# Decoding float64 weights: the exponent shift as a scaled copy on ScalarE, the sign on GpSimd, the residual on VectorE

## The chip, the cores and the metric

One core of a Trainium2 chip. The metric is the device time of one execution in microseconds; the kernel before took 1084.58 us in the median of 3 runs (1082.89 to 1086.86).

## The reference

The input is 2304 tokens (4 sequences of 576), 8 heads of 64, model width 512. Three layers follow one another:

```python
scores = scale * q @ k.T                 # causal window of 128, a linear bias per head
attn = softmax(scores) @ v
h = x @ w_in;  r = relu(h);  y = (r * r) @ w_out          # w_in 512x2048, w_out 2048x512
logits = y @ w_gate + softplus(y @ w_noise) * noise
out = sum over the top 2 of 8 experts of weight * (relu(y @ w1[e]) @ w2[e])   # 512x1024, 1024x512
```

The weights w_in and w_out of the middle layer reach the kernel as float64 (seen there as pairs of int32 words); all else is float32.

## The kernel before

TensorE multiplies in a float32 form that keeps fewer bits, so every operand is split in two: a high part that ScalarE writes by a Copy into that form, and a low part that is the number less its high part. A product is then three matmuls (high by high, high by low, low by high). `mm1` (L123, matmuls at L128) is the first product of a layer, `mm2` (L131, L133) the second.

The middle layer's weights come in 16 chunks. `load_w_moe(f)` (L99) brings chunk f in two halves, u = 0 and 1, of 128 x 512 numbers, 32 halves in all. One half is a 512 KB transfer on SyncE's queue (L104) into `st`, whose words alternate: the low and the high 32 bits of each float64, so that `lo` and `hi` are read with a step of two words. From them the float32 `a` is made: L108 shifts the high word by 3 and masks it (mantissa and low exponent bits), L109 puts the sign and the top exponent bit in, L111 the three topmost bits of the low word. ScalarE squares the high word, read as a float32 (L114), and L115 multiplies `a` by whether that square reaches a bound, so that numbers under float32's range come out as 0. ScalarE copies `a` into the high part of `w` (L116) and GpSimd subtracts to give the low part (L117). `st` and `a` have three buffers each.

The work is one stream per engine. The program's order is that of the loops below, but the framework moves instructions of one engine past one another where the data allow it, before the program runs; on the chip each engine takes its queue in order. First the attention for the first two token tiles runs, with the weights of chunks 0 and 1 (L630 to L636). Then the loop at L641 takes step s from 0 to 19: `m_mm1` (L335) multiplies chunk s for token group 0 (256 tokens) and chunk s - 4 for group 1, chunk s + 2 is loaded and decoded (L646), the attention of the next token tiles is spread over the steps, and `m_mm2` (L350) does the second product of the step before. Inside `m_mm1` ScalarE makes the ReLU, its square and the high part of that (L342 to L344), and VectorE the low part (L345). Weights stay in on-chip memory, so the groups from 2 on (L669) decode nothing. Attention's instructions that the text names: the subtraction for the keys (L218), the scaling and the subtraction for the queries on GpSimd (L223, L226), the masked maximum (L264, L267), the division by the sum (L277 on GpSimd, L282 on ScalarE), the transposes (L290). L137 to L168 make constants, some with GpSimd's iota.

Of the kernel before, what the change touches and what calls it, by code (L numbers as in the profile page):

```python
# [8 lines left out]
F32 = mybir.dt.float32  # L9
# [4 lines left out]
AF = mybir.ActivationFunctionType  # L14
OP = mybir.AluOpType
# [7 lines left out]
def kernel(  # L23
# [11 lines left out]
    nc = tc.nc  # L35
# [24 lines left out]
    BIG = -2.56e11  # L60


    TINY = (1.0625 * 2.0 ** -15) ** 2

    const = ctx.enter_context(tc.tile_pool(name="const", bufs=1))
    dram = ctx.enter_context(tc.tile_pool(name="dram", bufs=1, space=bass.MemoryType.DRAM))
# [19 lines left out]
    def slot():  # L86
        pool = ring_a if nslot[0] // HR % 2 == 0 else ring_b
        nslot[0] += 1
        return pool.tile([P, 2, 2 * DM], F32R, name="w")

    def load_w(src):
        w = slot()
        st = m2.tile([P, 2 * DM], F32, name="wst", bufs=2)
        nc.sync.dma_start(out=st, in_=src)
        nc.scalar.activation(w[:, 0], st, AF.Copy)  # L95
        nc.vector.tensor_tensor(out=w[:, 1], in0=st, in1=w[:, 0].bitcast(F32), op=OP.subtract)  # L96
        return w

    def load_w_moe(f):  # L99
        w = slot()  # L100
        for u in range(2):
            c = slice(u * DM, (u + 1) * DM)
            st = s64.tile([P, DM, 2], I32, name="w64", bufs=3)
            nc.sync.dma_start(out=st.rearrange("p f t -> p (f t)"), in_=wm32[f, u])  # L104
            lo, hi = st[:, :, 0], st[:, :, 1]
            a = s64.tile([P, DM], I32, name="wa", bufs=3)
            af = a.bitcast(F32)
            nc.vector.tensor_scalar(a, hi, 3, 0x3FFFFFF8, op0=OP.logical_shift_left, op1=OP.bitwise_and)  # L108
            nc.vector.scalar_tensor_tensor(out=a, in0=hi, scalar=-0x40000000, in1=a,  # L109
                                           op0=OP.bitwise_and, op1=OP.bitwise_or)  # L110
            nc.vector.scalar_tensor_tensor(out=a, in0=lo, scalar=29, in1=a,  # L111
                                           op0=OP.logical_shift_right, op1=OP.bitwise_or)
            m = hi.bitcast(F32)
            nc.scalar.activation(m, m, AF.Square)  # L114
            nc.vector.scalar_tensor_tensor(out=af, in0=m, scalar=TINY, in1=af, op0=OP.is_ge, op1=OP.mult)  # L115
            nc.scalar.activation(w[:, 0, c], af, AF.Copy)  # L116
            nc.gpsimd.tensor_tensor(out=w[:, 1, c], in0=af, in1=w[:, 0, c].bitcast(F32), op=OP.subtract)  # L117
        slots["m", f] = w

    def load_w_exp(e, f):  # L120
# [510 lines left out]
    for _, i, j, fn in sorted(steps, key=lambda x: x[:3]):  # L631
        fn()
        if j == 0 and i + 2 < FT:
            a_load(i + 2)
        if j == 3:
            load_w_moe(i)  # L636
# [4 lines left out]
    for s in range(NFC + LATE):  # L641
        now = [(g, s - LATE * g) for g in range(2) if 0 <= s - LATE * g < NFC]
        for g, f in now:
            m_mm1(g, f)
        if s + 2 < NFC:
            load_w_moe(s + 2)  # L646
        if s < NA:
            for fn in afill[s * per:(s + 1) * per]:
                fn()
        if s == NA - 1:  # L650
            A["cm"].__exit__(None, None, None)
            ring_b = ctx.enter_context(tc.tile_pool(name="ring_b", bufs=HR, side="right", reuse_waits="tile"))
            a_pool("at", 2, qk=1, v=2, qt=1, sb=2, pt=1)
            a_load(FT - 1)
            a_qk(FT - 1, "k")
            a_load(FT)
            afill2 = a_pair(FT, False)
        elif s >= OFF and s - OFF < len(afill2) and afill2[s - OFF]:
            afill2[s - OFF]()
        for g, f in prev:  # L660
            m_mm2(g, f)
        prev = now
        if s == NFC - 1:
            s64_cm.__exit__(None, None, None)
            gp_cm = tc.tile_pool(name="gp", bufs=1)
            gp = gp_cm.__enter__()
# [100 lines left out]
    with tc.For_i(0, nov, 1) as t:  # L767
        with tc.For_i(0, E, 1) as e:
# [6 lines left out]
            for dst, src in ((xg, yd[:, :]), (old, out)):  # L775
                nc.gpsimd.indirect_dma_start(
                    out=dst, out_offset=None, in_=src,
# [12 lines left out]
            for f in range(NEC):  # L790
                w = load_w(w_flat[ds((e * NEC + f) * P, P), :])
# [6 lines left out]
                                               op0=OP.max, op1=OP.subtract)  # L798
# [3 lines left out]
                out=out, out_offset=bass.IndirectOffsetOnAxis(ap=ic[:, 0:1], axis=0),  # L802
# [59 lines left out]
```

## Time and profile before

| | before |
|---|---|
| median of 3 runs | 1084.58 us (1082.89 to 1086.86) |
| profiled execution | 1080.51 us |
| its span, first to last instruction | 1078.5 us |
| TensorE busy (matmul) | 1019.0 us |
| VectorE busy | 593.5 us |
| ScalarE busy | 508.8 us |
| GpSimd busy | 236.2 us |
| mean granted TensorE clock | 0.989 |

In the profile PE is TensorE, DVE is VectorE, ACT is ScalarE, POOL is GpSimd and SP is SyncE; PEld is the loading of a matmul's weights. A busy time is the sum of an engine's instructions over the span; the engines run beside one another. A letter q behind an engine's name (SPq) is its sequencer or queue. Each row names a line of the kernel, an engine, an operation, what is written and read (out<-in) and the shapes, partitions x elements per partition.

### The profile page before, as it was taken

The numbers are of one execution on the slowest core, as the hardware profiler recorded it, in microseconds if no ns is written. First come the engines' busy times: TensorE is split into PE (matmuls) and PEld (weight loads), VectorE is DVE, ScalarE is ACT, GpSimd is POOL, SyncE is SP. The second block draws the span as 40 slices with busy tenths as digits, with TensorE's granted clock in tenths as the row PEclk, the third lists the DMA queues.
The fourth block names the chain that finished last, engine by engine and source line by source line (L and its number), as shares of the span: only waits on it lengthen the run. The fifth ranks groups of instructions, "written<-read, shape, count | busy, mean of one in ns | idle before, by whom it ended". The sixth has DMA issues, their size and how long they took to land.

```text
span 1078.5 us, 17965 instructions
## 1 busy us (share of the span) xinstructions
PE 1019.0 (94%) x6636; PEld 879.8 (82%) x6636; DVE 593.5 (55%) x1732; ACT 508.8 (47%) x1272; POOL 236.2 (22%) x219
## 2 busy tenths in 40 slices
PE   4788989999999999999999998999999999999997
PEld 3657768778888888888887787898888898888885
DVE  8999994576555646555547555444343444342312
ACT  6776665655646556665647525333322232321110
POOL 2334341220201111110100103314141322222111
PEclk9998999999999999999999999999999999999999
DMA  6333441621011111110015605535353444432111
GB/s 231 101 118 119 136 128 61 228 60 31 30 31 50 30 40 40 40 30 31 12 59 152 211 17 178 183 104 168 98 169 117 146 126 132 145 105 71 40 51 46
DMA packets 36521, 104.18 MB, mean 97 GB/s; under 512 B 7527, under 2 KB 7783, under 8 KB 36432
## 3 DMA queue, kind: packets, MB, share of 16 engines
q1 hardware_dynamic: 27232, 75.72, 22.3%
q0 software_dynamic: 9200, 27.29, 8.0%
q8 instruction: 53, 0.87, 0.3%
q14 instruction: 36, 0.29, 0.1%
HBM read 86.02 MB, written 20.00 MB: 98 GB/s over the span
## 4 chain that ended last, share of the span: by engine, by line
PE 65%; DVE 13%; DMA 8%; issue 6%; ACT 6%; POOL 1%; SPq 0%; POOLq 0%; DVEq 0%; ACTq 0%
PE h L128 28%; PE y L133 25%; DMA old<-out_dram,idx 4%; PE t L133 3%; PE t L305 2%; PE y L250 2%; DMA wst<-in_w_exp_dram 1%; DVE gl L345 1%; ACT sb L271 1%; DVE sb L264 1%; DVE wa L115 1%; PE t L569 1%; DMA qks<-in_qk_dram 1%; PE t L290 1%; DVE wa L109 1%
## 5 line engine op out<-in xcount | busy, mean ns | idle before, releaser
L128 PE MATMUL h<-xh,w 128*128 128x256 f32 x1152 | 238.3, 290 | 11.4 <-ACT r L342 6.3
L128 PE MATMUL h<-xeh,w 128*128 128x304 f32 (+2 forms) x1024 | 229.5, 305 | 0.9 <-ACT xeh L572 0.9
L128 PEld LDWEIGHTS h<-xh,w 128*128 128x128 f32 x1152 | 190.4, 193 | 22.8 <-ACT r L342 8.0
L133 PE MATMUL y<-w,gh 128*128 128x512 f32 x576 | 189.9, 410 | 0.9 <-ACT gh L344 0.8
L128 PEld LDWEIGHTS h<-xeh,w 128*128 128x128 f32 x1024 | 171.4, 188 | 3.5 <-ACT xeh L572 1.1
L128 PE MATMUL h<-xl,w 128*128 128x256 f32 x576 | 164.9, 286 | 1.1 <-DVE xl L312 1.1
L96 DVE TENSOR_TENSOR w<-wst,w 128x1024 fp32r<-128x1024 f32 x64 | 78.4, 1225 | 148.9 <-ACT w L95 148.8
L128 PE MATMUL h<-xel,w 128*128 128x304 f32 (+2 forms) x512 | 154.8, 302 | 0.4 <-DVE wt L574 0.4
L133 PE MATMUL y<-w,hh 128*128 128x512 f32 x464 | 145.0, 393 | 0.0
L95 ACT ACTIVATE w<-wst 128x1024 fp32r<-128x1024 f32 x64 | 67.7, 1058 | 135.8 <-PE t L133 128.0
L588 ACT ACTIVATE hh<-h 128x304 fp32r<-128x304 f32 (+1 forms) x120 | 50.4, 420 | 147.5 <-PE h L128 146.6
L133 PE MATMUL y<-w,gl 128*128 128x512 f32 x288 | 115.2, 402 | 3.2 <-DVE gl L345 3.2
L133 PEld LDWEIGHTS y<-w,gh 128*128 128x128 f32 x576 | 100.1, 191 | 21.1 <-ACT gh L344 1.3
L128 PEld LDWEIGHTS h<-xl,w 128*128 128x128 f32 x576 | 111.1, 193 | 4.9 <-DVE xl L312 1.3
L342 ACT ACTIVATE r<-h 128x256 f32<-128x256 f32 x144 | 54.3, 377 | 126.0 <-PE h L128 79.5
L345 DVE TENSOR_TENSOR gl<-r,gh 128x256 fp32r<-128x256 f32 x144 | 69.1, 480 | 79.1 <-ACT gh L344 78.3
L589 DVE SCALAR_TENSOR_TENSOR hl<-h,hh 128x304 fp32r<-128x304 f32 (+1 forms) x120 | 55.9, 466 | 102.2 <-ACT hh L588 102.1
L541 POOL DMA_INDIRECT xg<-yd,idx x40 | 40.8, 1021 | 273.2 <-PE h L128 111.8
L128 PEld LDWEIGHTS h<-xel,w 128*128 128x128 f32 x512 | 96.4, 188 | 1.8 <-DVE wt L574 0.6
L133 PEld LDWEIGHTS y<-w,hh 128*128 128x128 f32 x464 | 83.9, 188 | 14.8
L133 PE MATMUL y<-w,hl 128*128 128x512 f32 x232 | 91.3, 393 | 0.0
L277 POOL TENSOR_TENSOR sb<-sb,rs 128x512 f32<-128x512 f32 x28 | 29.8, 1063 | 276.0 <-ACT sb L253 106.4
(191 smaller groups left out, 1643.9 us busy)
## 6 DMA issues: line engine op xcount, KB each, us to landing
wst<-in_w_exp_dram SPq DMA_DIRECT2D x64, 512.0 KB, 3.7
w<-in_w_moe_dram SPq DMA_DIRECT2D x32, 512.0 KB, 3.7
qks<-in_qk_dram SPq DMA_DIRECT2D x20, 512.0 KB, 3.7
vs<-in_v_dram SPq DMA_DIRECT2D x20, 256.0 KB, 2.7
yd<-ysb SPq DMA_DIRECT2D x18, 256.0 KB, 2.1
out_dram<-ysb SPq DMA_DIRECT2D x1, 4608.0 KB, 14.0
xg<-yd,idx POOLq DMA_INDIRECT x40, 3.7
out_dram<-old,idx POOLq DMA_INDIRECT x29, 2.8
```

The lines of the kernel that those rows point to most:

```text
L95: nc.scalar.activation(w[:, 0], st, AF.Copy)
L96: nc.vector.tensor_tensor(out=w[:, 1], in0=st, in1=w[:, 0].bitcast(F32), op=OP.subtract)
L128: nc.tensor.matmul(ps, w[:, wi, c], x[:, kk, :], start=(n == 0), stop=(n == 3 * KD - 1))
L133: nc.tensor.matmul(ps, g, w[:, wi, DM:], start=(start and n == 0), stop=(stop and n == 2))
L250: nc.tensor.matmul(sp[c][:, pp], a[r, p, :], b[r, p, s0:s0 + 2, :], start=(n == 0), stop=(n == 2))
L277: nc.gpsimd.tensor_tensor(out=sb, in0=sb, in1=r.to_broadcast([P, 2, 2, P]), op=OP.mult)
L305: nc.tensor.matmul(o[64 * c:64 * c + 64, pp, :], vv[n][:, 4 * hf + j, :], pts[n][:, j, :], start=(n == 0), stop=(n == 1))
L342: nc.scalar.activation(r, h, AF.Relu)
L345: nc.vector.tensor_tensor(out=gl, in0=r, in1=gh.bitcast(F32), op=OP.subtract)
L541: nc.gpsimd.indirect_dma_start(out=xg, out_offset=None, in_=yd[:rows, :], in_offset=col(e, t), bounds_check=rows - 1, oob_is_err=False)
L588: nc.scalar.activation(hh[:, c], ps, AF.Relu)
L589: nc.vector.scalar_tensor_tensor(out=hl[:, c], in0=ps, scalar=0.0, in1=hh[:, c].bitcast(F32), op0=OP.max, op1=OP.subtract)
```

## The change

Four of the seven operations of a half chunk change. ScalarE multiplies the high word, read as a float32, by 2^-112 and writes it to `a`: this moves its exponent to where the shift by 3 leaves float32's, and numbers under float32's range become 0. GpSimd multiplies the high word by 0.0 in place, which leaves only its sign. VectorE puts the topmost bits of the low word to the sign (in place of `lo`), shifts `a` by 3 and joins the two. ScalarE's copy to the high part stays, and the subtraction for the low part moves from GpSimd to VectorE.

```diff
-    TINY = (1.0625 * 2.0 ** -15) ** 2
+    REBIAS = 2.0 ** -112
...
-            nc.vector.tensor_scalar(a, hi, 3, 0x3FFFFFF8, op0=OP.logical_shift_left, op1=OP.bitwise_and)
-            nc.vector.scalar_tensor_tensor(out=a, in0=hi, scalar=-0x40000000, in1=a,
-                                           op0=OP.bitwise_and, op1=OP.bitwise_or)
-            nc.vector.scalar_tensor_tensor(out=a, in0=lo, scalar=29, in1=a,
+
+
+            nc.scalar.activation(af, hi.bitcast(F32), AF.Copy, scale=REBIAS)
+            nc.gpsimd.tensor_scalar(hi.bitcast(F32), hi.bitcast(F32), 0.0, None, op0=OP.mult)
+            nc.vector.scalar_tensor_tensor(out=lo, in0=lo, scalar=29, in1=hi,
                                            op0=OP.logical_shift_right, op1=OP.bitwise_or)
-            m = hi.bitcast(F32)
-            nc.scalar.activation(m, m, AF.Square)
-            nc.vector.scalar_tensor_tensor(out=af, in0=m, scalar=TINY, in1=af, op0=OP.is_ge, op1=OP.mult)
+            nc.vector.scalar_tensor_tensor(out=a, in0=a, scalar=3, in1=lo,
+                                           op0=OP.logical_shift_left, op1=OP.bitwise_or)
             nc.scalar.activation(w[:, 0, c], af, AF.Copy)
-            nc.gpsimd.tensor_tensor(out=w[:, 1, c], in0=af, in1=w[:, 0, c].bitcast(F32), op=OP.subtract)
+            nc.vector.tensor_tensor(out=w[:, 1, c], in0=af, in1=w[:, 0, c].bitcast(F32), op=OP.subtract)
```

## Rows read from the trace of the kernel before

**Rows 1.** The page: busy us (share of the span) and instructions of each engine.
```profile
PE 1019.0 (94%) x6636; PEld 879.8 (82%) x6636; DVE 593.5 (55%) x1732; ACT 508.8 (47%) x1272; POOL 236.2 (22%) x219
```
**Rows 2.** Busy us by stretch: start:end, length, engines, granted clock, DMA share, GB/s.
```profile
10.00:168.00 158.00, 125.71 (x774) 100.81 (x775) 153.76 (x355) 107.49 (x305) 60.47 (x45) 0.95 0.38 124
168.00:330.00 162.00, 158.18 (x1160) 135.11 (x1159) 93.57 (x376) 94.15 (x269) 24.52 (x28) 0.99 0.23 77
330.00:1078.50 748.50, 731.86 (x4682) 641.16 (x4680) 340.05 (x978) 302.26 (x690) 148.63 (x143) 1.00 0.30 93
```
**Rows 3.** VectorE's groups, 10 to 168 us: xcount | busy us, mean ns | idle before.
```profile
L115 DVE SCALAR_TENSOR_TENSOR wa<-w,wa 128x512 f32<-128x512 f32 x32 | 27.3, 859 | 0.1
L111 DVE SCALAR_TENSOR_TENSOR wa<-w,wa 128x512 int32<-128x512 int32 x32 | 26.2, 821 | 0.0
L109 DVE SCALAR_TENSOR_TENSOR wa<-w,wa 128x512 int32<-128x512 int32 x32 | 25.6, 804 | 0.0
L108 DVE TENSOR_SCALAR wa<-w 128x512 int32<-128x512 int32 x32 | 19.7, 619 | 0.0
L264 DVE CUSTOM_DVE_ANT_0 sb<-sb,relv 128x128 f32<-128x128 f32 x48 | 16.3, 382 | 0.0
L345 DVE TENSOR_TENSOR gl<-r,gh 128x256 fp32r<-128x256 f32 x24 | 14.6, 607 | 0.6 <-ACT gh L344 0.5
...
L218 DVE TENSOR_TENSOR ktl<-qks,kth 128x512 fp32r<-128x512 f32 x5 | 3.4, 685 | 0.1
```
**Rows 4.** Instructions on the weight tiles: ns min/median/max, first and last start us.
```profile
L108 DVE TENSOR_SCALAR wa<-w x32: 397/418/1527, 16.2 to 161.8; 128x512 int32<-128x512 int32 x32
L109 DVE SCALAR_TENSOR_TENSOR wa<-w,wa x32: 658/682/1783, 17.4 to 162.7; 128x512 int32<-128x512 int32 x32
...
L114 ACT ACTIVATE w<-w x32: 646/676/727, 21.9 to 163.8; 128x512 f32<-128x512 f32 x32
...
L116 ACT ACTIVATE w<-wa x32: 612/631/634, 26.1 to 166.6; 128x512 fp32r<-128x512 f32 x32
L117 POOL TENSOR_TENSOR w<-wa,w x32: 1273/1353/2547, 26.8 to 168.0; 128x512 fp32r<-128x512 f32 x32
```
**Rows 5.** Lines 345 and 264, 10 to 168 us: ns min/median/max, first and last start.
```profile
L345 DVE TENSOR_TENSOR gl<-r,gh x24: 389/415/1522, 46.4 to 166.4; 128x256 fp32r<-128x256 f32 x24
...
L264 DVE CUSTOM_DVE_ANT_0 sb<-sb,relv x48: 260/283/1392, 12.6 to 160.5; 128x128 f32<-128x128 f32 x48
```
**Rows 6.** VectorE's instructions in order of time: start us, us it took.
```profile
112.25 0.68 DVE L109 SCALAR_TENSOR_TENSOR wa<-w,wa 128x512 int32<-128x512 int32 x1
112.85 0.42 DVE L108 TENSOR_SCALAR wa<-w 128x512 int32<-128x512 int32 x1
113.19 0.16 DVE L273 TENSOR_SCALAR sm<-sm 128x4 f32<-128x4 f32 x1
...
116.92 1.52 DVE L108 TENSOR_SCALAR wa<-w 128x512 int32<-128x512 int32 x1
```
**Rows 7.** GpSimd in order of time, the idle time before it in brackets.
```profile
116.80 1.35 POOL L117 TENSOR_TENSOR w<-wa,w 128x512 fp32r<-128x512 f32 x1 [1.29 <-ACT w L116]
```
**Rows 8.** GpSimd's groups over the whole span: xcount | busy us, mean ns.
```profile
L117 POOL TENSOR_TENSOR w<-wa,w 128x512 fp32r<-128x512 f32 x32 | 46.3, 1455 | 59.7 <-ACT w L116 59.7
...
L223 POOL TENSOR_TENSOR qks<-qks,qscale 128x512 f32<-128x512 f32 x17 | 18.4, 1081 | 46.4 <-DMA qks<-in_qk_dram 40.9 <-DVE sm L273 2.7 <-DVE relv L152 1.9
...
L163 POOL IOTA io<- 128x152 f32 x1 | 0.3, 258 | 0.0
...
L165 POOL IOTA pid<- 128x1 f32 x1 | 0.1, 137 | 0.0
```
**Rows 9.** Waits, 10 to 168 us: us in total, times, longest us.
```profile
DVE gl L345 <- ACT gh L344: 0.5, 1, 0.5
...
PE h L128 <- ACT r L342: 6.3, 5, 3.2
```
**Rows 10.** Waits of SyncE's queue up to 168 us, the same columns.
```profile
SPq L104 <- DVE wa L115: 81.4, 19, 9.4
```

## The prediction

> **What bounds the kernel now.** I read the page's table of busy times first: TensorE is busy for 94% of the span and VectorE for 55% [rows 1]. That is a mean over unlike stages, so the table by stage comes next [rows 2]. From 10 to 168 us, the stretch in which the 32 half chunks of float64 weights are decoded, VectorE is busy for 153.8 of 158.0 us, TensorE for 125.7, ScalarE for 107.5 and GpSimd for 60.5. After 168 us TensorE has 158.2 of 162.0 us and then 731.9 of 748.5 us, with VectorE at about half. So VectorE is the limit while weights are decoded and TensorE is the limit behind that. Nothing that the change touches runs after 168 us; what it is worth is read from those 158 us, and what the stretch gives or takes moves all that follows.
>
> Third, the groups of VectorE in the stretch [rows 3]: the four decode operations hold 27.3 + 26.2 + 25.6 + 19.7 = 98.8 us, 64% of its busy time. Their means (859, 821, 804, 619 ns) stand far above their medians, 682 ns for L109 (L111 and L115 have the same) and 418 ns for L108 [rows 4]. The timeline tells why: at 116.80 us GpSimd begins a 1.35 us subtraction [rows 7], and the L108 that VectorE starts at 116.92 takes 1.52 us [rows 6]. A GpSimd tensor operation holds VectorE up. In the waits, VectorE waits almost for nothing in the stretch [rows 9]: it has a backlog.
>
> **The change, part by part.** Per half chunk, on VectorE, it takes away one tensor_scalar and three scalar_tensor_tensor and adds two scalar_tensor_tensor and one tensor_tensor; on ScalarE a scaled Copy stands for the Square; on GpSimd a tensor_scalar stands for the 128x512 subtraction.
>
> VectorE's own work. What one operation costs in a queue without gaps is the distance to the next start: 0.34 us for an L108 (112.85 to 113.19) and 0.60 us for an L109 (112.25 to 112.85) [rows 6]. Removed: 0.34 + 3 x 0.60 = 2.14 us. Added: two at 0.60, and the dense subtraction, whose form has 685 ns [rows 3], at 0.61: 1.81 us. That is 0.33 us less per half, 10.6 us over 32. One operand is unproven: the first new operation reads two and writes one tensor with a word left out between any two. L109 reads one such tensor at 682 ns against 685 for the dense form, so a source costs nothing. For the output the bounds are none, and the halving of the rate that the rival below has; I take none, by L114, which reads and writes so on ScalarE at 676 ns against 631 for the dense L116 [rows 4].
>
> GpSimd's hold on VectorE. The excess of mean over median in the stretch is 177 + 139 + 122 + 201 = 639 ns per half, 20.4 us; with 24 x (607 - 415) ns = 4.6 us on L345 and 48 x (382 - 283) ns = 4.8 us on L264 [rows 3, 5] it is 29.8 us. GpSimd was busy for 60.5 us [rows 2], so each of its microseconds costs VectorE 0.49. The subtraction, 46.3 us [rows 8], thus costs 22.7 us, which go. The new tensor_scalar has no row. From below, a GpSimd operation that reads no tensor takes 137 ns at 1 element and 258 at 152 [rows 8], 0.80 ns for each more, so 0.55 us at 512. From above, the subtraction with two dense inputs has a median of 1.35 us [rows 4]; nearer is L223 at 1.08, whose second input repeats one number per 128 [rows 8]. I take the middle of the two ends, 0.95 us: 32 x 0.95 x 0.49 = 14.9 us, a gain of 7.8 us. The ends give 14.1 and 1.5 us.
>
> A rule speaks on this term. The Trainium skill, "SBUF — State Buffer", section "Who interferes with whom", says that a VectorE operation with two SBUF inputs is fully blocked by a GpSimd operation that reads SBUF, for as long as that lasts. The rows agree on the block for a single operation (1.52 for 0.42 us) and give 0.49 over all, as VectorE also has other operations to run. By a block of the whole duration the term would be 46.3 - 30.4 = 15.9 us in place of 7.8, and the forecast about 5 us lower.
>
> ScalarE: the scaled Copy lies between 631 and 676 ns [rows 4], at most 1.4 us less over 32; ScalarE is busy for 107.5 of 158.0 us, so I cost it at nothing. If that cover were gone it would be worth those 1.4 us. The Copy needs only the landed weights.
>
> Waits and queues. The first new VectorE operation waits for GpSimd, and the subtraction for ScalarE's Copy; behind either waits all of VectorE's queue: the residual L345, for which ScalarE and TensorE wait, and the attention's operations. The subtraction leaves GpSimd's queue, and the sign taken earlier stands there with L223, L226 and L277, which it delays by less than the subtraction did. The weight transfers on SyncE wait for a decoded buffer, 81.4 us in 19 waits [rows 10]; the buffer is now given back by the second VectorE operation, and those loads run two steps ahead, so I cost this at nothing. Its price, if the cover goes, is VectorE idle at the head of a half. No transfer is added, moved or taken away.
>
> The sum: 10.6 + 7.8 = 18.4 us off VectorE's 153.8. TensorE would then have 125.7 us to do in some 140, about 90% against 80% now, and starts to wait for ScalarE (6.3 us on L342 already [rows 9]) more than for VectorE. Of VectorE's saving I take two thirds, 12.3 us, with a half and the whole as the ends. The profiled execution took 1080.5 us around a span of 1078.5, so 1068.2; the median of the runs shown is 1084.6, 0.38% above, which gives **1072**. The ends, 12.1 x 1/2 = 6 and 24.7 us, give 1060 to 1079.
>
> **The rivals.** A measurement of this kernel can tell about 0.3%, 3.3 us, from no change.
>
> First, slower: the two new waits empty VectorE's queue. If nothing else is ready, a half chunk waits 0.63 us for the Copy and 0.95 us for the sign: 32 x 1.58 = 50.6 us against 18.4 gained. It decides at 18.4 / 32 = 0.58 us per half. At half of the full waits, 0.79 us, the time grows by 25.3 - 18.4 = 6.9 us, to 1091. Against it speaks that L345, also a subtraction behind a ScalarE Copy, waited 0.5 us in all over 24 times [rows 9], and that other work (attention, another half) is queued; for it, that the chain through the decode is now longer by GpSimd's step. 14%.
>
> Second, GpSimd's tensor_scalar is slow. Saving and loss meet at (10.6 + 22.7) / (32 x 0.49) = 2.12 us. At 2.6 us, nearly twice the subtraction's median, it is 40.8 - 33.3 = 7.5 us slower: 1092. For it speaks that no row shows the operation; against, that it reads one tensor where the subtraction reads two. 6%.
>
> Third, no change that can be told: the output with gaps halves VectorE's rate. Going from 418 to 682 ns [rows 4] costs 264 ns for half the rate; halving it again would cost 528 ns, 16.9 us over 32, leaving 1.5 of the 18.4 us: about 1083. The Trainium skill, "Vector Engine (DVE) Microarchitecture Reference", section "Measured stream behaviour on trn2", says that a port streams at its full rate only over runs of at least two adjacent words. This output has no such runs; for a source without them L109 shows no loss [rows 4]. The same time comes if TensorE or ScalarE, and not VectorE's sum, sets the stretch. 14%.
>
> Fourth, more than forecast: a GpSimd operation with one input doesn't hold VectorE at all. Then 10.6 + 22.7 = 33.3 us go from VectorE; TensorE's idle time in the stretch is 158.0 - 125.7 = 32.3 us, and two thirds of 33.3 give 1058. 8%.
>
> That the change doesn't do what it says is hardly open: each operation can be counted.
>
> **How the numbers follow.** The forecast has 58%. Faster by over 0.3%: 58 + 8 = 66%; within it: 14%; slower: 14 + 6 = 20%. The range is 1059 to 1090: it holds the forecast's ends, the third rival, and the milder part of the first; left out are the second, the worse half of the first and most of the fourth, under 2 in 10. The forecast alone has 1060 to 1079.
>
> **What would show it.** In the profile after, right: the decode stretch ends at some 156 us; VectorE's three decode groups stand near 690 ns in the median, with means under those of now; GpSimd's tensor_scalar lies between 0.55 and 1.35 us; VectorE is still over 90% busy in the stretch and TensorE's share there has grown; from the end of the stretch to the end of the span nothing has changed. Wrong: idle time of VectorE ahead of the sign or the Copy of over 0.58 us per half; a tensor_scalar over 2.1 us; the first operation at 1.2 us; or a stretch that shrinks by VectorE's 18 us or by none.

## The result and the profile after

| | before | after |
|---|---|---|
| median of 4 runs each | 1083.86 us (1082.89 to 1086.86) | 1071.95 us (1071.78 to 1073.84) |
| profiled execution | 1080.51 us | 1073.84 us |
| its span | 1078.5 us | 1072.1 us |
| VectorE busy | 593.5 us | 569.1 us |
| GpSimd busy | 236.2 us | 245.2 us |

The ratio is 0.9892 with an interval of 0.9869 to 0.9915: 11.9 us faster. The two profiled executions are only 6.7 us apart, since the one before lies 3.4 us under its median and the one after 1.9 us above; the traces are read for where time goes, the medians for how much.

The same table by stage as in [rows 2], for the kernel after: the stretch with the decode in it (it ends at 151 us, before at 169), and the 17 us behind.

```profile
10.00:153.00 143.00, 115.76 (x731) 93.23 (x732) 128.51 (x317) 103.41 (x298) 70.03 (x44) 0.94 0.42 137
153.00:170.00 17.00, 17.00 (x119) 15.15 (x118) 6.10 (x13) 8.03 (x22) 1.04 (x1) 1.00 0.00 1
```

VectorE has 128.5 us of work where it had 153.8, GpSimd 70.0 where it had 60.5. TensorE is busy for all of the 17 us from 153 on; before, it was busy for 12.7 of the same 17. VectorE is idle for 14.5 of these 143 us; before it was for 4.2 of 158.

Most of the 18 us come back behind the decode. From its end to the end of the span, before and then after:

```profile
169.30:1078.50 909.20, 888.73 (x5834) 775.26 (x5832) 432.70 (x1352) 395.99 (x957) 171.86 (x168) 1.00 0.29 90
151.40:1072.10 920.70, 897.04 (x5896) 782.46 (x5894) 435.19 (x1360) 401.19 (x974) 172.89 (x169) 1.00 0.28 89
```

The first count is TensorE's matmuls: 62 more of the 6636 are still to do, and what follows takes 11.5 us longer.

The decode's operations after, as in [rows 4] (ns min/median/max, first and last start us):

```profile
L110 ACT ACTIVATE wa<-w x32: 646/664/704, 10.5 to 142.9; 128x512 f32<-128x512 f32 x32
L111 POOL TENSOR_SCALAR w<-w x32: 1545/1626/2097, 11.3 to 143.8; 128x512 f32<-128x512 f32 x32
L112 DVE SCALAR_TENSOR_TENSOR w<-w x32: 675/694/1770, 17.7 to 146.1; 128x512 int32<-128x512 int32 x32
L114 DVE SCALAR_TENSOR_TENSOR wa<-wa,w x32: 676/684/1752, 19.0 to 146.8; 128x512 int32<-128x512 int32 x32
L116 ACT ACTIVATE w<-wa x32: 612/620/636, 22.0 to 148.0; 128x512 fp32r<-128x512 f32 x32
L117 DVE TENSOR_TENSOR w<-wa,w x32: 655/681/1528, 25.1 to 150.7; 128x512 fp32r<-128x512 f32 x32
```

L110 is the scaled Copy, L111 the sign on GpSimd, L112 and L114 the two bit operations, L117 the subtraction. VectorE's three are as costed: even L112, with its gaps in the output, has a median only 10 ns above that of L114. GpSimd's operation is not: 1.63 us, longer than the two-input subtraction that it replaces (1.35).

VectorE's groups from 10 to 153 us, as in [rows 3]:

```profile
L112 DVE SCALAR_TENSOR_TENSOR w<-w 128x512 int32<-128x512 int32 x32 | 29.9, 935 | 5.4 <-POOL w L111 5.0
L114 DVE SCALAR_TENSOR_TENSOR wa<-wa,w 128x512 int32<-128x512 int32 x32 | 23.9, 758 | 0.5 <-ACT xh L311 0.5
L117 DVE TENSOR_TENSOR w<-wa,w 128x512 fp32r<-128x512 f32 x32 | 23.0, 730 | 0.1
L264 DVE CUSTOM_DVE_ANT_0 sb<-sb,relv 128x128 f32<-128x128 f32 x48 | 13.8, 333 | 0.0
L345 DVE TENSOR_TENSOR gl<-r,gh 128x256 fp32r<-128x256 f32 x22 | 11.4, 520 | 2.2 <-ACT gh L344 1.9 <-PE y L133 0.3
```

The decode takes 76.8 us of VectorE; before it took 98.8 [rows 3]. The excess of mean over median is 241 + 74 + 49 ns per half, 11.7 us, and with L345 (median 418) 2.2 us and L264 (median 282) 2.4 us in all 16.3 us; before it was 29.8. One new wait is there: L112 for GpSimd's sign, 5.0 us.

### The profile page after: what moved, and what is told of

Same layout as the page of the kernel before. It is cut to its first block, busy times and chain, and to the rows that moved or that the text cites. A ratio compares the mean times of both kernels' runs of the same rounds, so it can differ in the third digit from the quotient of the medians.

```text
span 1072.1 us, 17953 instructions
## 1 busy us (share of the span) xinstructions
PE 1014.4 (95%) x6636; PEld 876.9 (82%) x6636; DVE 569.1 (53%) x1700; ACT 507.7 (47%) x1272; POOL 245.2 (23%) x219
## 4 chain that ended last, share of the span: by engine, by line
PE 69%; DVE 9%; DMA 8%; issue 6%; ACT 6%; POOL 1%; SPq 0%; POOLq 0%; ACTq 0%; DVEq 0%
PE h L128 30%; PE y L133 27%; DMA old<-out_dram,idx 4%; PE t L133 3%; PE t L305 3%; PE y L250 2%; PE t L569 1%; PE t L290 1%; DMA qks<-in_qk_dram 1%; ACT sb L271 1%; DMA xg<-yd,idx 1%; DVE gl L345 1%; DVE sb L264 1%; DVE w L112 1%; POOL w L111 1%
## 5 line engine op out<-in xcount | busy, mean ns | idle before, releaser
L96 DVE TENSOR_TENSOR w<-wst,w 128x1024 fp32r<-128x1024 f32 x64 | 78.4, 1226 | 148.5 <-ACT w L95 148.4
L345 DVE TENSOR_TENSOR gl<-r,gh 128x256 fp32r<-128x256 f32 x144 | 66.5, 461 | 83.2 <-ACT gh L344 82.3
L133 PEld LDWEIGHTS y<-w,hh 128*128 128x128 f32 x464 | 83.9, 188 | 14.9
L277 POOL TENSOR_TENSOR sb<-sb,rs 128x512 f32<-128x512 f32 x28 | 29.8, 1064 | 273.9 <-ACT sb L253 130.4
## 6 DMA issues: line engine op xcount, KB each, us to landing
out_dram<-ysb SPq DMA_DIRECT2D x1, 4608.0 KB, 14.2
```

The lines of the kernel that those rows point to most:

```text
L133: nc.tensor.matmul(ps, g, w[:, wi, DM:], start=(start and n == 0), stop=(stop and n == 2))
L277: nc.gpsimd.tensor_tensor(out=sb, in0=sb, in1=r.to_broadcast([P, 2, 2, P]), op=OP.mult)
L345: nc.vector.tensor_tensor(out=gl, in0=r, in1=gh.bitcast(F32), op=OP.subtract)
```

## The experiments

Nine kernels, each beside the kernel before on the same chip. That kernel had a median of 1083.9 us beside the first four runs of the table, 1083.6 beside the next three, and 1081.1 beside the last two, which are therefore compared by their distance from it. The changed kernel has 1071.95 us, a ratio of 0.9892; all edits are to it but for the third, and the last two also have the edit of the first. The last two columns are read from the profiled execution: when the last subtraction of the decode starts (150.7 in the changed kernel, 168.0 before), and the matmuls that TensorE does from 10 to 170 us (848 and 785).

| run | median us | ratio to before (95%) | VectorE busy us | GpSimd busy us | last subtraction, us | matmuls, 10 to 170 us |
|---|---|---|---|---|---|---|
| sign on VectorE | 1067.3 | 0.9853 (0.9827 to 0.9879) | 569.0 | 190.1 | 148.4 | 904 |
| residual back on GpSimd | 1097.3 | 1.0124 (1.0099 to 1.0148) | 569.0 | 288.2 | 159.1 | 693 |
| before, residual on VectorE | 1077.8 | 0.9939 (0.9917 to 0.9960) | 585.7 | 190.9 | 165.0 | 829 |
| one bit operation left out | 1073.8 | 0.9904 (0.9882 to 0.9925) | 546.7 | 241.0 | 137.0 | 844 |
| sign on ScalarE | 1429.1 | 1.3192 (1.3154 to 1.3230) | 673.6 | 214.5 | 145.4 | 913 |
| a second GpSimd operation | 1088.0 | 1.0036 (1.0017 to 1.0055) | 578.4 | 301.2 | 165.8 | 742 |
| subtraction done twice | 1085.3 | 1.0016 (0.9994 to 1.0039) | 585.5 | 242.1 | 172.8 | 775 |
| sign on VectorE, one bit operation left out | 1057.3 | 0.9787 (0.9760 to 0.9814) | 549.4 | 191.4 | 123.1 | 958 |
| sign on VectorE, GpSimd beside it | 1078.7 | 0.9979 (0.9966 to 0.9992) | 579.8 | 247.9 | 163.7 | 791 |

Sign on ScalarE apart, which does other work behind the decode, the ratios of all these kernels, the changed one and the one before among them, stand in the order of the matmuls done by 170 us, from 693 (slowest) to 958 (fastest). They do not stand in the order of VectorE's busy time (569 us for three kernels between 1067 and 1097) nor of the decode's end.

### One part of the change alone

```diff
 # the kernel before
-            nc.gpsimd.tensor_tensor(out=w[:, 1, c], in0=af, in1=w[:, 0, c].bitcast(F32), op=OP.subtract)
+            nc.vector.tensor_tensor(out=w[:, 1, c], in0=af, in1=w[:, 0, c].bitcast(F32), op=OP.subtract)
```

> The kernel before with one part of the change alone: the subtraction for the low part on VectorE in place of GpSimd, all else as before. Theory 1: VectorE gains 32 x 0.60 = 19.2 us of operations and loses the hold of the 32 subtractions, 22.7 us, so its busy time stays within 5 us of 593 and the time is 1078 to 1087 us. Rival (the hold costs nothing): VectorE's 19 us more lengthen the stretch, and the time is 1094 us or more.

Measured: 1077.8 us, 6.1 us under the kernel before (1083.9), VectorE 7.8 us less busy though it does 32 subtractions more. Both are a little beyond theory 1 (within 5 us of 593, and 1078 at the least), on the side away from the rival. Its groups from 10 to 168 us in this kernel:

```profile
L115 DVE SCALAR_TENSOR_TENSOR wa<-w,wa 128x512 f32<-128x512 f32 x32 | 26.0, 821 | 0.3 <-ACT w L114 0.2
L111 DVE SCALAR_TENSOR_TENSOR wa<-w,wa 128x512 int32<-128x512 int32 x32 | 21.6, 680 | 0.0
L117 DVE TENSOR_TENSOR w<-wa,w 128x512 fp32r<-128x512 f32 x32 | 21.4, 682 | 1.4 <-ACT w L116 1.2
L109 DVE SCALAR_TENSOR_TENSOR wa<-w,wa 128x512 int32<-128x512 int32 x32 | 21.2, 681 | 0.0
L108 DVE TENSOR_SCALAR wa<-w 128x512 int32<-128x512 int32 x32 | 14.6, 472 | 0.0
L264 DVE CUSTOM_DVE_ANT_0 sb<-sb,relv 128x128 f32<-128x128 f32 x48 | 12.5, 307 | 0.0
L345 DVE TENSOR_TENSOR gl<-r,gh 128x256 fp32r<-128x256 f32 x26 | 10.8, 415 | 1.5 <-ACT gh L344 1.5
```

L109 and L111 fell from 804 and 821 ns [rows 3] to their median. What is left over the medians (683, 417 and 282 ns for L115, L108 and L264) is 4.4 + 1.8 + 1.2 = 7.4 us, so the 32 subtractions on GpSimd had cost VectorE 29.8 - 7.4 = 22.4 us; the prediction had 22.7. The rival that the hold costs nothing falls. This part alone gives half of the change's gain: here the subtraction is cheaper on the crowded engine than beside it. The other half is the rest of the change, which no run has by itself.

### The sign, moved to VectorE and to ScalarE

```diff
-            nc.gpsimd.tensor_scalar(hi.bitcast(F32), hi.bitcast(F32), 0.0, None, op0=OP.mult)
+            nc.vector.tensor_scalar(hi, hi, -0x80000000, None, op0=OP.bitwise_and)
```

> The changed kernel with one step altered: VectorE and not GpSimd takes the sign (a bitwise and in place, one input), so GpSimd has no part in the decode. Theory 1 (VectorE's sum sets the decode stretch, and what GpSimd's reads hold it up counts in that sum): 32 x 0.34 = 10.9 us of operations are added, the hold of the 32 tensor_scalar, 16.3 us by mean over median in the changed kernel, goes, and so do the 5.0 us that VectorE waited for the sign; VectorE busy falls by some 5 us against the changed kernel's 569, and the time lies between 1065 and 1072 us. Rival (only the count of VectorE's operations matters, the hold falls into time that it would have waited anyway): 10.9 us more on VectorE, and 1077 to 1083 us.

Measured: 1067.3 us (1066.99 to 1071.44), all five runs under the fastest of the changed kernel's four. VectorE is as busy as in the changed kernel (569.0 against 569.1), not 5 us less: 32 x 0.34 = 10.9 us came, and the excess over the medians fell from 16.3 to 6.3 us. What is left of it stands mostly in two groups (their medians are 685 and 686 ns):

```profile
L117 DVE TENSOR_TENSOR w<-wa,w 128x512 fp32r<-128x512 f32 x32 | 25.0, 788 | 1.3 <-ACT w L116 0.9
L112 DVE SCALAR_TENSOR_TENSOR w<-w 128x512 int32<-128x512 int32 x32 | 23.2, 734 | 0.0
```

The time lies in theory 1's range, but it did not come from VectorE's sum; what is gone is the wait for the sign, and GpSimd's use. The stretch from 10 to 170 us, TensorE's matmuls as the first count, in the changed kernel and then in this one:

```profile
10.00:170.00 160.00, 132.76 (x848) 108.38 (x849) 134.61 (x330) 111.44 (x318) 71.07 (x45) 0.95 0.38 122
```
```profile
10.00:170.00 160.00, 139.82 (x904) 115.69 (x905) 136.77 (x373) 114.02 (x327) 16.49 (x18) 0.87 0.39 128
```

56 more matmuls are done by 170 us, at a lower granted clock (0.87 against 0.95) even.

```diff
-            nc.gpsimd.tensor_scalar(hi.bitcast(F32), hi.bitcast(F32), 0.0, None, op0=OP.mult)
+            nc.scalar.activation(hi.bitcast(F32), hi.bitcast(F32), AF.Copy, scale=0.0)
```

> The changed kernel with the sign taken by ScalarE (a Copy scaled by 0.0 in place) and not by GpSimd. Theory 1: the hold of 16.3 us goes from VectorE, no operation is added to it, and ScalarE rises by 32 x 0.66 = 21 us to some 125 of the 143 us of the stretch, still under VectorE; about 1066 us (1062 to 1070). Rival (ScalarE, which carries the chain from the first product to the second, becomes the bound): 1076 us or more, with TensorE's waits for ScalarE's ReLU and its square well over those of the changed kernel.

Measured: 1429.1 us, which tells nothing of the change: this kernel no longer computes the reference. It runs 7628 matmuls in all, 6636 in the others, as it would if tokens went to other experts and the loop for experts with too many tokens ran; the edit is the sign, so the weights' signs are the likely cause, but they were not read. The stretch up to 170 us, ahead of the experts, has the same work:

```profile
10.00:170.00 160.00, 144.36 (x913) 117.41 (x914) 125.78 (x340) 128.67 (x361) 16.02 (x17) 0.94 0.42 131
```

913 matmuls by 170 us, with ScalarE busy for 128.7 of 160 us: about as far as the kernel with the sign on VectorE (904). ScalarE didn't become the bound there; how much the whole would have gained stays open.

### The residual back on GpSimd, and a second operation there

```diff
-            nc.vector.tensor_tensor(out=w[:, 1, c], in0=af, in1=w[:, 0, c].bitcast(F32), op=OP.subtract)
+            nc.gpsimd.tensor_tensor(out=w[:, 1, c], in0=af, in1=w[:, 0, c].bitcast(F32), op=OP.subtract)
```

> The changed kernel with the subtraction for the low part left on GpSimd: VectorE has only the two bit operations of a half. Theory 1: 32 x 0.60 = 19.2 us go from VectorE, and the hold of 32 two-input subtractions comes back; that was 22.7 us by the price of the kernel before, so the time lies within 1068 to 1077 us, beside the changed kernel's 1072. Rival (only the count of VectorE's operations matters): VectorE falls by 19 us and the time to 1062 or less.

Measured: 1097.3 us, 25 us over the changed kernel and beyond both expectations. VectorE does 19 us less of operations and is as busy as before the edit (569.0): the hold has filled the gap. And it waits more; in the waits of this kernel, for VectorE and for GpSimd:

```profile
DVE w L112 <- POOL w L111: 16.6, 14, 3.0
```
```profile
POOL w L117 <- ACT w L116: 21.1, 18, 6.9
```

GpSimd waits at the subtraction for ScalarE's Copy for 21.1 us, and the sign of the next half stands behind it in the same queue; VectorE waits for that sign. Theory 1 had the hold but not this: GpSimd in order at both ends of one chain. How the 25 us divide between the hold and the waits is not shown.

```diff
             nc.gpsimd.tensor_scalar(hi.bitcast(F32), hi.bitcast(F32), 0.0, None, op0=OP.mult)
+            nc.gpsimd.tensor_scalar(w[:, 0, c], hi.bitcast(F32), 0.0, None, op0=OP.mult)
```

> The changed kernel with a second tensor_scalar on GpSimd per half, which reads the sign's words and writes them where the high part is written later, so that its result is not used. Theory 1: each reads 512 numbers and holds VectorE up by some 0.45 us where it meets an operation with two inputs there; 32 of them add 10 to 16 us of mean over median to VectorE, and the time rises by 4 to 10 us, to 1076 to 1082. Rival (a one-input operation holds nothing up): no change in VectorE's busy time, and 1071 to 1074 us unless VectorE waits longer for the sign.

Measured: 1088.0 us, 16 us over the changed kernel. VectorE's busy time rose by 9.3 us and its wait for the sign from 5.0 to 12.7 us:

```profile
DVE w L113 <- POOL w L111: 12.7, 13, 2.9
```

The direction is as in theory 1, the size is larger (1082 was its end); the second operation stands ahead of the next sign in GpSimd's queue, and the longer wait may be the rest. This run doesn't part hold from wait; the last one nearly does.

### VectorE's slack: one operation more, one less

```diff
             nc.vector.tensor_tensor(out=w[:, 1, c], in0=af, in1=w[:, 0, c].bitcast(F32), op=OP.subtract)
+            nc.vector.tensor_tensor(out=w[:, 1, c], in0=af, in1=w[:, 0, c].bitcast(F32), op=OP.subtract)
```

> The changed kernel with the subtraction for the low part done twice on VectorE, the second like the first. Theory 1: 32 x 0.60 = 19.2 us more on VectorE; the stretch is VectorE's, so the time rises by a half to all of it, to 1081 to 1091 us. Rival (VectorE has slack behind the change): under 1077 us.

Measured: 1085.3 us, 13.4 us more for 16.4 us more on VectorE. As theory 1 has it, there is no slack upwards.

```diff
-            nc.vector.scalar_tensor_tensor(out=lo, in0=lo, scalar=29, in1=hi,
-                                           op0=OP.logical_shift_right, op1=OP.bitwise_or)
-            nc.vector.scalar_tensor_tensor(out=a, in0=a, scalar=3, in1=lo,
+            nc.vector.scalar_tensor_tensor(out=a, in0=a, scalar=3, in1=hi,
```

> The changed kernel without the first bit operation on VectorE: the three lowest mantissa bits of the weights are left out, and the second operation takes the sign directly. Theory 1 (VectorE still sets the stretch, and its microseconds turn into time at about one half, as 24.3 us less gave 11.9): 32 x 0.60 = 19.2 us less on VectorE, and about 1062 us (1058 to 1066). Rival (after the change TensorE and the chain through the engines set the stretch): VectorE 19 us lower and the time above 1069 us.

Measured: 1073.8 us, no gain, for 22.4 us less on VectorE. Theory 1 had 1062 and missed; the rival's number came. The waits of VectorE in this kernel (10 to 170 us), its last subtraction, and its stretch:

```profile
DVE wa L112 <- POOL w L111: 16.6, 19, 1.9
DVE gl L343 <- ACT gh L342: 9.9, 8, 1.9
```
```profile
L115 DVE TENSOR_TENSOR w<-wa,w x32: 649/682/1283, 25.1 to 137.0; 128x512 fp32r<-128x512 f32 x32
```
```profile
10.00:170.00 160.00, 129.52 (x844) 107.18 (x845) 112.86 (x297) 110.78 (x319) 67.80 (x45) 0.96 0.38 123
```

With less to do VectorE waits for GpSimd's sign for 16.6 us, where it was 5.0; in all it is idle for 47.1 of the 160 us, where it was 25.4. Even so the decode ends 14 us sooner than in the changed kernel (137.0 against 150.7); it is TensorE that is no further at 170 us, with 844 matmuls against 848. So the same operation was left out of the kernel in which VectorE takes the sign:

> The kernel with VectorE taking the sign (1067.3 us), without the first bit operation: the three lowest mantissa bits of the weights are left out, as in the run that left them out of the changed kernel. That run gained nothing although VectorE had 22 us less to do. Theory A (there the wait for GpSimd's sign, 16.6 us in place of 5.0, took the gain): without GpSimd in the decode 19.2 us less on VectorE give about a half, 1055 to 1061 us. Theory B (VectorE has slack behind the change, TensorE and the order of the steps set the stretch): 1064 us or more.

Measured: 1057.3 us beside 1081.1 for the kernel before, 23.8 us under it; the kernel with the sign on VectorE is 16.6 us under its own (1067.3 beside 1083.9). So 7.2 us are gained, not the 10.0 between the two medians, for 19.6 us less on VectorE. The two intervals of the ratio (0.9760 to 0.9814, 0.9827 to 0.9879) are apart, so without GpSimd in the decode VectorE's saving is worth something again, about a third. That fits Theory A; on the scale of 1083.9 the time would be 1060, inside A's range and 4 us under B's. That the wait for the sign had taken the gain is not shown: this run takes away GpSimd's hold with the wait, and in the run before it the decode was not what came late.

### Hold or wait

The kernel with the sign on VectorE, and beside it an operation on GpSimd that VectorE never waits for:

```diff
             nc.vector.tensor_scalar(hi, hi, -0x80000000, None, op0=OP.bitwise_and)
+            nc.gpsimd.tensor_scalar(w[:, 0, c], hi.bitcast(F32), 0.0, None, op0=OP.mult)
```

> The kernel with VectorE taking the sign (1067.3 us), and beside it a GpSimd tensor_scalar per half whose result is not used: it reads the sign's words and writes where ScalarE writes the high part later. VectorE waits for none of them. It tells the hold from the wait for the sign. If the hold is what GpSimd's 32 operations cost the changed kernel: VectorE's mean over median grows by 12 to 20 us, and the time to 1073 to 1082 us. If the wait for the sign is: within 3 us of 1067.

Measured: 1078.7 us, 2.4 us under the kernel before beside it (1081.1), where the kernel without that operation is 16.6 us under: 14.2 us more, with VectorE 10.8 us busier (579.8 against 569.0). The excess of mean over median is 18.2 us, 12 us more and so at the low end of what was expected; most of it stands in three groups (medians 685, 683 and 682 ns):

```profile
L118 DVE TENSOR_TENSOR w<-wa,w 128x512 fp32r<-128x512 f32 x32 | 26.4, 831 | 3.4 <-ACT w L117 3.0
L113 DVE SCALAR_TENSOR_TENSOR w<-w 128x512 int32<-128x512 int32 x32 | 26.3, 832 | 0.0
L115 DVE SCALAR_TENSOR_TENSOR wa<-wa,w 128x512 int32<-128x512 int32 x32 | 25.1, 790 | 0.0
```

VectorE waits for none of the added operations directly. ScalarE's Copy, which writes the same place behind them, waits 1.9 us for one of them, and VectorE 3.0 us for that Copy (0.9 without). So the hold is the main cost, with a small part of waiting in it. GpSimd in order of time in this kernel, then VectorE:

```profile
116.09 1.33 POOL L278 TENSOR_TENSOR sb<-sb,rs 128x512 f32<-128x512 f32 x1 [0.39 <-ACT w L117]
118.40 1.89 POOL L112 TENSOR_SCALAR w<-w 128x512 fp32r<-128x512 f32 x1 [0.98 <-DVE w L111]
```
```profile
116.44 1.53 DVE L118 TENSOR_TENSOR w<-wa,w 128x512 fp32r<-128x512 f32 x1
117.89 0.42 DVE L111 TENSOR_SCALAR w<-w 128x512 int32<-128x512 int32 x1
118.22 0.68 DVE L118 TENSOR_TENSOR w<-wa,w 128x512 fp32r<-128x512 f32 x1
118.83 0.85 DVE L346 TENSOR_TENSOR gl<-r,gh 128x256 fp32r<-128x256 f32 x1
119.60 0.68 DVE L113 SCALAR_TENSOR_TENSOR w<-w 128x512 int32<-128x512 int32 x1
```

A GpSimd operation with two inputs, 1.33 us long, stretches the subtraction L118 from 0.68 to 1.53 us, by 0.85. One with one input, 1.89 us long, stretches L346 from its median of 0.42 to 0.85, by 0.43, and then L113 runs at its usual 0.68 us while GpSimd is still busy. The same comes out of the timelines when each GpSimd operation is set beside the VectorE operations that it overlaps: of 22 signs of the changed kernel that stand singly there, none adds more than 0.49 us over the medians, and of 21 subtractions of the kernel before eleven add 1.07 to 1.11. So the hold does not go with GpSimd's duration. A price per number read would fit, but only one form with one input was run, so that is argued and not shown.

## Why the prediction came out

**The stage and the engine.** Right: what the change did it did in the decode, which ends 18 us earlier, and VectorE was the limit there: 13.4 us for the subtraction done twice, 14.2 us for the hold put back. The text had its end at some 156 us; it was 151. VectorE is 89.9% busy from 10 to 153 us, just under the forecast's 90%.

**VectorE's own work, 10.6 us.** Right. The medians of the three new operations (694, 684, 681 ns) are those that the text took from L109 and L218, and of the 24.4 us that VectorE lost 10.9 are left beside the hold's 13.5. The third rival's price, 528 ns for an output with gaps, was 10 ns. The rule on adjacent words that the text set beside that rival (the Trainium skill, "Vector Engine (DVE) Microarchitecture Reference", "Measured stream behaviour on trn2") doesn't show for this step of two words: L112 has it in both inputs and in the output and takes 694 ns, L114 684.

**GpSimd's hold, 7.8 us.** This term of the sum was too small: it measured 29.8 - 16.3 = 13.5 us, inside the text's ends of 1.5 and 14.1. The step had two halves. What the subtraction had cost was put at 22.7 us and measured at 22.4. What the tensor_scalar would cost was put at 14.9 us, as 0.95 us "the middle of the two ends" times "each of its microseconds costs VectorE 0.49". Both factors failed, in opposite directions: the operation takes a mean of 1.74 us, above both ends, and a microsecond of GpSimd's in the stretch after costs 16.3 / 70.0 = 0.23. That 0.23 still counts what the attention's operations on GpSimd cost: 6.3 of the 16.3 us stay when GpSimd has no part in the decode. So the 32 signs cost 10.0 us, 0.31 each where the text had 0.47; in the run that put such an operation back by itself VectorE's busy time rose by 10.8 us, 0.34 each. A mean over two-input operations was no price for one with one input.

**The second rival**, a slow tensor_scalar, had the direction of the duration right (1.63 us, where it needed 2.12 to matter) and the consequence wrong for the same reason: such an operation held VectorE up by no more than 0.49 us in the changed kernel.

**The rule of a block for as long as the operation lasts** (the Trainium skill, "SBUF — State Buffer", "Who interferes with whom") was weighed against 0.49. For a GpSimd operation with one input it is not borne out: 0.43 us beside one of 1.89 us, and L113, which has two inputs, at its usual time while that one runs. For two inputs the rows come near it: when L118 began, L278 had 0.98 us left to run, and L118 was held up by 0.85. The row on which the text said that the two agree (1.52 for 0.42 us) is no case of the rule, since L108 has one input.

**The sum and its conversion.** VectorE lost 24.4 us of busy time where the sum had 18.4, and the time fell by 11.9, which is 0.49 of it where "of VectorE's saving I take two thirds". The two errors cancel: 12.3 us forecast, 11.9 measured, and that the number came so close is luck. The two thirds had a reason, that TensorE would do its 125.7 us in some 140, about 90%, and then wait for ScalarE more than for VectorE, with nothing changed behind the stretch. This did not come. TensorE is busy for 81% of the time from 10 to 153 us. Its waits from 10 to 170 us are 9.6 us for ScalarE and 18.4 for VectorE, where they were 16.2 and 14.8. The stretch shrank by 18 us, which the text had named as a sign of being wrong, and 11.5 of them came back behind it, 8.3 as busy time of TensorE (897.0 against 888.7), which had fewer matmuls done when the decode ended. Nor is the half a rate that carries over: the operation left out gave about 7 of 19.6 us without GpSimd in the decode and nothing of 22.4 with it. More work on VectorE costs more than less gives back, 13.4 for 16.4 us: it was at 90%, and downwards its idle time grows, 14.5 us in the stretch where it had been 4.2.

**The fourth rival's time** has a slip: two thirds of 33.3 us, with the 0.38% that the forecast adds, give 1062 and not 1058, so a kernel without any hold would have lain inside the forecast's own 1060 to 1079, and the time alone could not have told the two apart. The hold of the signs, 10 to 11 us, does.

**The waits.** Two were feared. The wait for ScalarE's Copy didn't come (0.1 us ahead of L117). The wait for the sign did, 5.0 us, a quarter of the 0.58 us per half at which it would have turned the result. It was not free, though: with the sign on VectorE, at the same busy time, the kernel is 4.7 us faster (with medians of 1083.9 us for the kernel before beside both). That run takes away this wait together with GpSimd's load, so how the 4.7 us divide between the wait and what GpSimd does to the attention's own operations is not shown.

## What to carry to other kernels

Work moved to GpSimd to relieve VectorE can come back as longer operations on VectorE; here, where VectorE was the limit, a 0.34 us operation of its own was cheaper than a GpSimd operation beside it. Compare mean and median of one form on VectorE: in these kernels the difference was what GpSimd cost it, and it did not go with GpSimd's duration. Before an operation is judged worthless because leaving it out gained nothing, look which waits have grown. And where one engine limits a stretch and another all that follows, count what the second has done by a fixed time: here that, and not the end of the stretch, ordered the kernels.

## What had not been expected of the hardware

A one-input multiplication on GpSimd (128 x 512 float32, a step of two words) takes 1.63 us, longer than a dense two-input subtraction there, 1.35 us, and yet holds VectorE up half as much. Multiplying by 0.0 on GpSimd leaves the sign, as the changed kernel needs it; with the same product on ScalarE the kernel no longer computes the reference (whether the zero loses its sign there was not looked at by itself). The fastest kernel of the study with the whole computation is the change with the sign on VectorE, 1067.3 us.
